# Selecting the first rows with a 0/1 matrix on TensorE instead of moving them by DMA, in the start of a convolution and feed-forward kernel

## The chip, the cores and the metric

The kernel runs on one core of one Trainium2 chip. The metric is the device time of one execution in microseconds (us). It was compared in rounds in which the kernel before and the kernel in question run in turn on the same chip. The profiled span is some 1.7 us shorter than the device time; spans are compared with spans only. "A draw" below is one profiled execution.

Engine names in the profile: PE is TensorE's matmuls, PEld its weight loads, DVE VectorE, ACT ScalarE, POOL GpSimd, SP SyncE; SPq and POOLq are where these two issue DMAs. "Block" is a piece of work of the main loop: block 0 and block 1 are one sub-block of 512 tokens each, later blocks are two.

## The reference, cut to what matters

```python
# attention-like part: a causal convolution whose 7 weights differ per token and head
w = softmax(weight_gen, axis=-1)               # (8, 4096, 8 heads, 7)
out[b, s, h*24 + g] = sum_k w[b, s, h, k] * x_pad[b, s + k, h*24 + g]   # D = 192
# feed-forward part on 32768 tokens
h = maximum(out @ w_in, 0.0)                   # w_in (192, 2048)
return (h * h) @ w_out                         # w_out (2048, 192)
```

## The kernel before: the parts that matter

The convolution is done as matmuls with banded matrices. For each sub-block there are five tiles of 128 rows of softmax weights (`wr`), laid one token to a partition. DVE multiplies them with a mask into bands (`bd`), and TensorE multiplies the bands with x. The softmax of the first 1024 tokens leaves its weights `v` with 8 tokens to a partition, so for block 0 small DMAs move the rows into tiles:

```python
def wr_load_sbuf(j, parts, order, engines):
    wr_t[j] = p_wr.tile([P, NT, HP, SL * 2], f16, name="wr")
    ...                                  # one DMA per tile, alternating over engines
        engines[n % len(engines)].dma_start(out=wr_t[j][..., i], in_=s.v[...])
```

A "unit" is 12 short matmuls (`h`, output 64x256) with 128 columns of w_in in blocks 0 and 1; ACT then applies ReLU (`t`), and DVE squares (`g`). A second copy of w_in with its halves of partitions exchanged (`w_i[:, q, 1]`) lets two row groups of the array work side by side. For the first half of the columns (q = 0) TensorE makes that copy with an exchange matrix; for the second half (q = 1) two DMAs, the "crossing", make it. Unit 4 is the first that needs the second half.

The start, in program order:

```python
spin(25)                                  # filler matmuls: they warm TensorE, no result
half_swap(); band_mask()
nc.gpsimd.memset(v_big, 0.0)
s0.load(nc.sync)                          # weight_gen of the first softmax
load_w_in(w_st[0], 0, nc.sync)            # first half of w_in, float32
x_load_f32(0)                             # x of block 0
load_w_in(w_st[1], 1, nc.sync)            # second half of w_in
... s0.exp / total / recip / scale        # v
nc.scalar.copy(out=w_i[:, 0, 0], in_=w_st[0])
wr_load_sbuf(0, [s0], (0, 2, 1, 4, 3), (nc.sync, nc.gpsimd))
wr_load_sbuf(1, [s0], range(NT), (nc.gpsimd,))
x_cast(0, nc.scalar.copy)
cross_w_in_by_pe(0)
spin(14)                                  # 14 more fillers
x_load_f32(1)
nc.scalar.copy(out=w_i[:, 1, 0], in_=w_st[1])
cross_w_in(1)                             # the crossing, by DMA
s1.load(nc.sync)
for i in (0, 2, 1, 3, 4):
    st_band(0, (i,))
st_conv(0)
nc.gpsimd.tensor_copy(out=gate, in_=x_st[1][:, 0:1])   # holds w_out back until x of block 1 is there
for q in range(4):
    load_w_out(q, 4)
```

The softmax here doesn't subtract the row's maximum and nothing guards it: scores larger than these inputs give would overflow.

## Time and profile before

| what | value |
|---|---|
| time, median of 3 runs | 736.59 us (735.5 to 736.84) |
| span in the profile, TensorE busy | 734.8 us, 725.9 us |
| first ReLU | 17.64 us |
| crossing issued / load of w_out issued | 14.01 / 15.37 us |
| unit 4 starts, its ReLU (the fifth) | 20.68 us, without a wait for data / 22.79 us |
| convolution of block 2 starts | 34.37 us |

The prediction below shows the page's totals, the waits and the timeline of the start. These are stretches of two microseconds of the kernel before; the columns are the stretch, its length, busy time and number of instructions of PE, PEld, DVE, ACT and POOL, the clock granted to TensorE (1.00 is full), the busy share of the 16 DMA engines and GB/s:

```profile
10.00:12.00 2.00, 2.00 (x10) 0.88 (x10) 0.00 (x0) 2.00 (x3) 2.00 (x5) 1.00 0.50 95
12.00:14.00 2.00, 1.97 (x21) 0.76 (x22) 1.23 (x3) 1.76 (x2) 0.22 (x1) 1.00 0.86 241
...
22.00:24.00 2.00, 1.62 (x26) 1.36 (x27) 1.93 (x6) 2.00 (x4) 0.00 (x0) 1.00 1.47 231
```

From 10 to 14 us TensorE is busy for all but 0.03 us, because of the 14 fillers and the matmuls of w_in's exchange, and the clock is full. From 22 us the DMA engines have more than they can do at once (a share over 1 means that packets overlap on an engine).

### The profile page before, as it was taken

How to read it: one execution, taken by the hardware profiler on the slowest of the kernel's cores; microseconds unless marked ns; L12 is line 12 of the kernel's file. 1: busy time of each engine (PE TensorE's matmuls, PEld its weight loads, DVE VectorE, ACT ScalarE, POOL GpSimd, SP SyncE). 2: the span in 40 equal slices, each digit the busy share in tenths (PEclk: the TensorE clock that was granted, in tenths of full speed). 3: DMA queues.
4: the chain of work that ended last, by engine and by line, in shares of the span. 5: the costliest groups of instructions: out<-in, count | busy, mean ns of one | idle time of the engine just before them, and what ended most of it. 6: DMA issues, size and time to landing. Idle time of an engine off the chain costs nothing.

```text
span 734.8 us, 31124 instructions
## 1 busy us (share of the span) xinstructions
PE 725.9 (99%) x14106; PEld 529.4 (72%) x14106; DVE 627.3 (85%) x856; ACT 613.5 (83%) x724; POOL 100.2 (14%) x148
## 2 busy tenths in 40 slices
PE   7999999999999999999999999999999999999998
PEld 3767777777767777777777777777777777777777
DVE  5999898998899988889888889888889888778853
ACT  4998888988888888888888888888888888888883
POOL 7322222320001100011000110010100110001000
PEclk9999999999999999999999999999999999999999
DMA  7846444794444533454433554334544315444012
GB/s 210 130 81 138 80 62 104 144 165 120 92 74 99 122 76 73 66 137 100 80 65 76 116 124 85 59 64 127 103 87 83 61 48 121 66 87 78 29 45 66
DMA packets 126544, 68.71 MB, mean 93 GB/s; under 512 B 85193, under 2 KB 122636, under 8 KB 125900
## 3 DMA queue, kind: packets, MB, share of 16 engines
q1 hardware_dynamic: 80908, 48.12, 22.9%
q0 software_dynamic: 45360, 18.50, 21.6%
q8 instruction: 110, 1.80, 1.0%
q14 instruction: 22, 0.18, 0.1%
q10 hardware_dynamic: 144, 0.10, 0.0%
HBM read 50.18 MB, written 28.70 MB: 107 GB/s over the span
## 4 chain that ended last, share of the span: by engine, by line
PE 70%; DVE 0%; ACT 0%; issue 0%
PE o L560 35%; PE h L518 32%; PE yp L450 3%; DVE g L536 0%; ACT o_sb L574 0%
## 5 line engine op out<-in xcount | busy, mean ns | idle before, releaser
L532 ACT ACTIVATE t<-h 128x1024 f16<-128x1024 f32 x512 | 496.4, 1026 | 60.1 <-PE h L518 59.7
L560 PEld LDWEIGHTS <-g 64*128 64x128 f16 (+1 forms) x8032 | 342.8, 94 | 56.9 <-issue 2.5
L560 PE MATMUL o<-w_o,g 64*128 64x192 f16 (+1 forms) x8032 | 379.7, 243 | 0.7 <-DVE g L536 0.6
L536 DVE TENSOR_TENSOR g<-t 128x2048 f16<-128x2048 f16 (+1 forms) x309 | 309.2, 1037 | 27.6 <-ACT t L532 27.3
L518 PE MATMUL h<-y,w_p 64*128 64x512 f16 x2400 | 291.7, 376 | 0.0
L518 PEld LDWEIGHTS <-w_p 64*128 64x128 f16 x2400 | 113.8, 94 | 94.8
L381 DVE TENSOR_TENSOR bd<-wr,mask 128x4160 f16<-128x4160 f16 (+3 forms) x89 | 149.4, 1703 | 4.7 <-DMA wr<-v_first 4.7
L576 DVE TENSOR_TENSOR o_sb<-o,o_sb 128x384 f32<-128x384 f32 x123 | 68.4, 556 | 62.1 <-ACT o_sb L574 61.3
L333 POOL DMA_DIRECT2D xt<-in_x_dram x62 | 52.1, 844 | 422.6 <-PE yp L450 363.7
L574 ACT COPY o_sb<-o 128x384 f32<-128x384 f32 x129 | 61.5, 477 | 48.0 <-PE o L560 47.5
L518 PE MATMUL h<-y,w_i 64*128 64x512 f16 (+1 forms) x768 | 82.3, 350 | 1.8 <-ACT t L532 0.8
L518 PEld LDWEIGHTS <-w_i 64*128 64x128 f16 x768 | 37.2, 94 | 27.7 <-issue 4.0
L450 PEld LDWEIGHTS <-xt 128*32 128x32 f16 x2000 | 24.4, 95 | 10.6 <-issue 10.6
L272 DVE TENSOR_TENSOR v_big<-ex,rcp 128x112 f16<-128x112 f32 (+5 forms) x180 | 29.9, 237 | 2.1 <-DMA vd<-v_big 1.1
L460 DVE CAST y<-yp 128x1024 f16<-128x1024 f32 x25 | 30.4, 1218 | 0.0
L450 PE MATMUL yp<-bd,xt 128*32 128x104 f16 (+1 forms) x2000 | 28.3, 209 | 0.0
L250 ACT ACTIVATE ex<-wg 128x560 f32<-128x560 f32 (+4 forms) x38 | 25.9, 682 | 1.7 <-DMA wg<-in_weight_gen_dram 1.7
L257 DVE TENSOR_REDUCE ssum<-ex 128x80 f32<-128x560 f32 (+4 forms) x38 | 25.3, 666 | 2.2 <-ACT ex L250 2.2
L460 ACT CAST y<-yp 128x1024 f16<-128x1024 f32 x25 | 25.2, 1007 | 0.0
L264 DVE RECIPROCAL rcp<-ssum 128x80 f32<-128x80 f32 (+4 forms) x38 | 22.8, 600 | 1.3
L323 POOL DMA_DIRECT2D xt<-in_x_dram x7 | 3.9, 555 | 124.7 <-PE yp L450 109.7
L363 POOL DMA_DIRECT2D wr<-v_first x31 | 16.9, 565 | 15.9 <-DVE v_first L272 15.7
(34 smaller groups left out, 95.8 us busy)
## 6 DMA issues: line engine op xcount, KB each, us to landing
out_dram<-o_sb SPq DMA_DIRECT2D x63, 384.0 KB
xt<-in_x_dram POOLq DMA_DIRECT2D x42, 240.0 KB, 5.1
wg<-in_weight_gen_dram SPq DMA_DIRECT2D x4, 1064.0 KB
xt<-in_x_dram POOLq DMA_DIRECT2D x20, 192.0 KB, 4.6
wr<-vd SPq DMA_DIRECT2D x38, 80.0 KB
vd<-v_big SPq DMA_DIRECT2D x5, 512.0 KB
y<-y SPq DMA_DIRECT2D x100, 24.0 KB
wg<-in_weight_gen_dram SPq DMA_DIRECT2D x5, 392.0 KB
```

The costliest lines, as they stand in the source:

```text
L250: nc.scalar.activation(out=self.ex[:, lo:hi].rearrange("p r g k e -> p (r g) k e"), in_=self.wg[:, lo:hi].rearrange("p r (g e) k -> p (r g ...
L272: eng.tensor_tensor(out=bass.AP(tensor=v.tensor, offset=v.offset + lo * H * SL + lo % SL * 2 + g * SL * 2, ap=[list(v.ap[0]), [H * SL + 2, ...
L333: eng.dma_start(out=dst[:, first:last], in_=ap)
L381: nc.vector.tensor_tensor(out=bd_t[j][:, H * lo : H * (lo + len(tiles) * n)].rearrange("p (g m c) -> p g m c", g=shape[1], c=2 * SL), in0= ...
L450: nc.tensor.matmul(out=yp[p0 : p0 + 32, k - k0, a:b], lhsT=x_t[s][:, i, c0 : c0 + 32], rhs=bd[:, head // 2, e, 0 : b - a], start=True, sto ...
L460: copy(out=y[:, k0 : k0 + 2], in_=yp)
L518: nc.tensor.matmul(out=h[:, half, jj * th : (jj + 1) * th], lhsT=w_in_chunk(w, u * per + jj, slot, half), rhs=y_t[j][r0 : r0 + RT, k, 0:th ...
L532: nc.scalar.activation(out=t1[:, e], in_=h, func=ActF.Relu)
L536: nc.vector.tensor_tensor(out=g[:, a : e + 1], in0=t1[:, a : e + 1], in1=t1[:, a : e + 1], op=AluOp.mult)
L560: nc.tensor.matmul(out=oo[:, cc * Dm : (cc + 1) * Dm], lhsT=g[r0 : r0 + n, cc * P : (cc + 1) * P], rhs=w_o[r0 : r0 + n, fc, :], start=(fc ...
L574: nc.scalar.copy(out=o_sb, in_=o[0][:, c])
L576: nc.vector.tensor_tensor(out=o_sb, in0=o[1][:, c], in1=o_sb, op=AluOp.add)
```

## The change

Intent: take the DMA between v and the bands away. A 0/1 matrix `sel` picks the rows: eight matmuls per tile, one for each of the eight tokens of a partition, add up in PSUM, and ACT copies the 128x64 result out. x is loaded ahead of w_in. DVE, which no longer waits for rows, casts the first half of w_in and copies all of y; the 14 fillers go; ACT's cast of the second half of w_in comes last. Cut to its core:

```diff
+    def row_select():
+        nc.gpsimd.affine_select(out=sel, in_=sel, pattern=[[-1, NSEL]], ..., fill=1.0,
+                                base=FIRST - 1, channel_multiplier=FIRST)
+    def select_rows(j, s, tiles):
+        ...
+        for i in tiles:
+            a = max(j % NBB * TB + tile_start(j, i), 0) - s.t0
+            for r in range(s.r):
+                c = a + FIRST - 1 - r
+                nc.tensor.matmul(out=pr_t[j][:, i], lhsT=sel[:, c : c + P],
+                                 rhs=s.v[:, HALO + r]..., start=(r == 0), stop=(r == s.r - 1), ...)
+            nc.scalar.copy(out=wr_t[j][:, i]..., in_=pr_t[j][:, i])
@@ st_conv
-                copies = ((0, 2, nc.scalar.copy), (2, NK, nc.vector.tensor_copy))
+                copies = ((0, NK, nc.vector.tensor_copy),)
@@ start
+        row_select(); band_mask()
         half_swap()
-        band_mask()
+        x_load_f32(0)
         load_w_in(w_st[0], 0, nc.sync)
-        x_load_f32(0)
         load_w_in(w_st[1], 1, nc.sync)
...
-        nc.scalar.copy(out=w_i[:, 0, 0], in_=w_st[0])
-        wr_load_sbuf(0, [s0], (0, 2, 1, 4, 3), (nc.sync, nc.gpsimd))
-        wr_load_sbuf(1, [s0], range(NT), (nc.gpsimd,))
         x_cast(0, nc.scalar.copy)
-        cross_w_in_by_pe(0)
-        spin(14)
         x_load_f32(1)
+        nc.vector.tensor_copy(out=w_i[:, 0, 0], in_=w_st[0])
+        wr_load_sbuf(1, [s0], range(NT), (nc.gpsimd, nc.sync))
+        s1.load(nc.sync)
+        select_rows(0, s0, (0, 2, 1))
+        cross_w_in_by_pe(0, 0, 2 * TB)
+        select_rows(0, s0, (3, 4))
+        cross_w_in_by_pe(0, 2 * TB, 3 * TB)
         nc.scalar.copy(out=w_i[:, 1, 0], in_=w_st[1])
         cross_w_in(1)
-        s1.load(nc.sync)
```

## The prediction

> **What bounds the kernel now.** I read the page's totals and the chain that ended last, then TensorE's waits before and after 26 us, then the timeline of the first 18 us.
>
> ```profile
> span 734.8 us, 31124 instructions
> PE 725.9 (99%) x14106; PEld 529.4 (72%) x14106; DVE 627.3 (85%) x856; ACT 613.5 (83%) x724; POOL 100.2 (14%) x148
> PE 70%; DVE 0%; ACT 0%; issue 0%
> ```
>
> TensorE works in 725.9 of 734.8 us and the chain that ended last lies on it. Only 8.9 us of the span are without a matmul. The waits of TensorE from 26 us to the end of the span:
>
> ```profile
> PE o L560 <- DVE g L536: 0.6, 2, 0.3
> ```
>
> and from 0 to 26 us (total us, times, longest):
>
> ```profile
> PE pt L149 <- ACT w_i L643: 1.3, 1, 1.3
> PE wp L624 <- DVE warm L616: 1.3, 1, 1.3
> PE h L518 <- ACT t L532: 0.8, 1, 0.8
> PE h L518 <- ACT y L503: 0.7, 1, 0.7
> PE yp L487 <- DVE bd L381: 0.3, 1, 0.3
> PE yp L487 <- DVE xt L347: 0.3, 1, 0.3
> ```
>
> After 26 us TensorE has 0.6 us of waits in 709 us, so what the start-up gains or loses is passed through to the end one for one, and nothing else in this change touches the steady part. The waits of the start look small because 39 filler matmuls (wp, 25 and then 14) hide them: they do no work for the result. The real question is when the first useful unit (h, L518) can run. The timeline of the start (start us, duration us, engine, line):
>
> ```profile
> 6.61 1.46 DVE L272 TENSOR_TENSOR v_first<-ex,rcp 128x112 f16<-128x112 f32 x8
> 8.38 1.47 ACT L643 CAST w_i<-w_st 128x1536 f16<-128x1536 f32 x1 [3.70 <-DMA w_st<-in_moe_w_in_dram]
> 9.90 0.99 ACT L347 CAST xt<-x_st 128x960 f16<-128x960 f32 x1
> 10.79 1.49 ACT L153 CAST w_i<-pt 128x1024 f16<-128x1024 f32 x2
> 12.51 1.47 ACT L650 CAST w_i<-w_st 128x1536 f16<-128x1536 f32 x1 [0.23 <-DMA w_st<-in_moe_w_in_dram]
> 12.77 2.60 DVE L381 TENSOR_TENSOR bd<-wr,mask 128x832 f16<-128x832 f16 x5 [4.71 <-DMA wr<-v_first]
> 14.93 0.94 PE L487 MATMUL yp<-bd,xt 128*32 128x104 f16 x46 [0.28 <-DVE bd L381]
> 15.90 0.59 ACT L503 CAST y<-yp 128x512 f16<-128x512 f32 x1 [1.91 <-PE yp L487]
> 16.52 0.42 DVE L503 CAST y<-yp 128x256 f16<-128x256 f32 x1 [1.14 <-ACT y L503]
> 16.54 3.04 PE L518 MATMUL h<-y,w_i 64*128 64x256 f16 x48 [0.68 <-ACT y L503]
> 17.64 2.85 ACT L532 ACTIVATE t<-h 128x1024 f16<-128x1024 f32 x3 [1.16 <-PE h L518]
> ```
>
> The softmax weights v are ready at 6.61 + 1.46 = 8.07. DVE then idles 4.71 us for the row-moving DMAs, builds five bands, TensorE convolves until 15.87, y is copied out, and the first ReLU starts at 17.64. That last moment is my yardstick. From v to the first ReLU it is 17.64 - 8.07 = 9.57 us, and 4.70 of it is the DMA. One of those issues, of 8 to 9 us (KB, us to landing):
>
> ```profile
> wr<-v_first POOLq DMA_DIRECT2D x1, 16.0 KB, 4.5
> ```
>
> **What the Trainium skill says.** (1) "DMA: Bandwidth & Descriptors", section "Anatomy of one DMA — SWDGE (gpsimd) path", puts a fixed cost of about 2.0 us on a DMA, mostly completion. The trace agrees in kind: 16 KB takes 4.5 us here behind other traffic, so size is not what costs. (2) "TensorE: Matmul & The Clock Gate", "Back-to-back issue gap", gives about 81 ns for a weight load and matmul pair at N=128. Here a 16-pair group with N=192 takes 1.49 us, 93 ns each; nothing as short as N=64 with 128 columns of weights is in this trace. (3) The same page, "What's actually happening", says the clock falls to half after an idle window of about 3.4 us. In the trace the first fillers are 0.43 us apart and from 4.7 us on 0.21, so warming is seen; falling back is not seen in this run. (4) "PSUM — Partial Sum Buffer", "PSUM bank collisions raise a hardware error", asks that a bank, not an address, be guarded between engines. The trace agrees that copies out of one PSUM tile are kept apart: DVE's part of y waited 1.14 us, until ACT's part was done, although the two read different columns.
>
> **The change part by part.**
> *Removed: five DMAs of rows of block 0, and 14 fillers.* That takes away DVE's 4.71 us wait. The fillers were only filling (3.18 us, none on the path).
>
> *Added: 40 selecting matmuls (8 per tile, N=64) and 5 ACT copies of 128x64 out of PSUM.* Matmuls: between 60 and 80 ns per pair by (2), I take 70: 8 x 0.07 = 0.55 us per tile. ACT copies from PSUM cost 589 ns for 512 columns and 1006 for 1024 in this trace, that is 0.17 us + 0.815 ns per column, so 0.22 us for 64. All five tiles lie in one PSUM bank (5 x 64 x 4 B = 1280 B), so by (4) the matmuls of the next tile wait for the copy of the last one. With 0.1 us per hand-over, a tile then costs 0.55 + 0.1 + 0.22 + 0.1 = 0.97 us, one after the other, not 0.55.
>
> *Order on the engines.* The 25 fillers end at 1.27 + 7.29 = 8.56, so tile 0 starts there. Tile 1, the third, has its matmuls done at 8.56 + 2 x 0.97 + 0.55 = 11.05. Then two crossing matmuls (N=512, 0.22 each): 11.5. ACT copies their 1024 columns: 11.6 + 1.0 = 12.6; only then, in order, tile 3: 12.8. Tile 4: 12.9 + 0.55 + 0.1 + 0.22 = 13.8. Its band on DVE (0.59 mean of L381): 14.5. The convolution ended 0.49 after the last band (15.87 against 15.37): 15.0.
>
> *y by DVE alone.* DVE takes 424 ns for 256 columns from PSUM and 1218 for 1024, so 1.03 ns per column and 0.95 us for 768: 15.95. Before, the two copies in turn ended at 16.94, which is 1.07 after the convolution: about equal. From there the first ReLU came 17.64 - 16.94 = 0.70 later, so now at 16.65. Gain 17.64 - 16.65 = 1.0 us.
>
> *x ahead of w_in; casts moved.* x is 491 KB, each half of w_in 786 KB, weight_gen 401 KB. Over 2 to 10 us the queues moved about 290 GB/s. w_in's first half landed at 8.38; x put ahead delays it by at most 491/290 = 1.7 us, to 9.3 (they overlapped before) or 10.1. DVE's cast of 1536 columns is 653 ns x 1536/960 = 1.05 us, so done by 10.4 to 11.2. The crossing matmuls ask for it at 11.05, so this is nearly hidden. DVE's bands 0, 2, 1 stand behind this cast, but they have until 12.8. The ACT cast of x (0.99 us) goes to about 6 us, where ACT idles: hidden. What it saves is the 1.47 + 0.99 us that ACT spent ahead of the crossing copies, without which the copies of tiles could not be this early.
>
> *Second half of w_in.* ACT's cast moves behind tile 4's copy and the last crossing copy (0.59): 13.8 + 0.6 + 1.47 = 15.9 instead of 13.98. Its two DMAs are issued 1.9 us later.
>
> Sum: 4.7 us of DMA wait go, about 3.7 us come back as the select-copy chain with a crossing copy in its middle (v to last band, 8.07 to 14.5, instead of 8.07 to 15.37, with 0.49 of it spent on fillers). Net about -1.0 us, passed on: 736.6 - 1.0 = 735.6; I say 735.5.
>
> **Rivals.**
> A. *The tiles are not held apart by the bank.* Then tiles cost 0.55 each, tile 1's matmuls end at 10.2 and all is 0.9 us or more earlier: about 734.3. Against it: the wait of DVE's y for ACT's.
> B. *The clock falls back.* Between 8.56 and 16 us the full 512-column fillers are gone and TensorE has short matmuls with gaps of under 1 us. For: less work per us than before. Against: no gap near 3.4 us, and a 1.35 us gap at 8.56 did no harm before. If it fell, the first units (0.76 us each) would take 1.5, against 1.0 us of ReLU per unit: 1 to 1.5 us lost, about 736.8.
> C. *The second half of w_in comes late.* Unit 4 ran at 20.68 and is now wanted at 19.7; its DMAs, issued 15.9 to 17.1, may land at 19.5 to 20.5. But ACT only took that unit at 22.79, 1.3 us after it ended, so the wait is mostly absorbed: 0 to 0.5 us.
> D. *w_in's first half is later than 10.1.* DVE stands at its cast with the bands behind it, so each us beyond 10.1 costs nearly one us. With 3 us late the gain is gone. Against: the queue moves 1.68 MB (weight_gen, x, first half) by 8 us at the rates seen.
> E. *Rows of block 1 late.* POOL now has the larger selecting mask to make before its memset, so its DMAs start perhaps 1 to 2 us later and land at 14.5 to 15.5; they are wanted at 15.95. Within the slack.
>
> **Range and chances.** My sum gives -1.0 with about 0.5 either way from the pair time (60 or 80 ns: 24 to 32 pairs on the path, 0.3 us each way) and the hand-overs; A is worth up to -2.3, B to D up to +0.8. The three runs of before spread over 1.3 us themselves. So 735.5, with 734.0 to 737.0 for 8 in 10. 2% is 14.7 us, more than the whole start-up from v to the first ReLU (9.57 us), so neither side of it is in reach without a fault: 0.01 each.
>
> **What would show it.** The wait of 4.71 us on wr gone from DVE. Five groups of 8 selecting matmuls about 1 us apart (A: 0.55). An ACT copy of 0.22 us after each, the fourth standing behind a 1.0 us crossing copy. DVE's last band at 14 to 15 us, and the first ReLU at 16.65. The granted clock at 1.00 throughout, matmuls of L518 of 256 columns at about 269 ns as now (B: longer). After 26 us no new wait of TensorE. I am wrong if the first ReLU is not earlier, or is earlier by over 2 us, or if the steady part changes its length.

## The result, and the profile after

| | before | after |
|---|---|---|
| median of 6 runs each, same rounds | 736.25 us (735.49 to 738.67) | 738.39 us (737.74 to 739.45) |
| mean granted clock | 1.000 in the profiled run; 0.998 to 1.000 in the later rounds | 0.995 to 0.997 in the six runs |
| span in the profile | 734.8 us | 736.8 us |

The ratio is 1.0027, with a 95% interval of 1.001 to 1.0044. Ratios here are the mean time of one kernel's fast runs over that of the other's of the same rounds, so they are not quite the ratio of the medians. Within 2% it is the same time, as predicted, but the sign is wrong: the kernel is slower by about 2 us, and 738.39 lies above the predicted range.

The waits of TensorE in the kernel after, from 0 to 26 us (total, times, longest):

```profile
PE h L542 <- DMA w_i<-w_i: 2.2, 1, 2.2
PE pr L388 <- ACT wr L393: 1.6, 3, 1.0
...
PE h L542 <- DVE y L527: 1.0, 1, 1.0
PE pt L157 <- DVE w_i L671: 1.0, 1, 1.0
```

The first line was not there before: a unit waits 2.2 us for the crossing. The second is the hand-over between selecting matmuls and ACT's copies, as predicted. The last is TensorE waiting for DVE's cast of w_in. The timeline of the kernel after:

```profile
8.42 0.40 PE L388 MATMUL pr<-v_first,sel 128*128 128x64 f16 x8
...
9.11 0.39 PE L388 MATMUL pr<-v_first,sel 128*128 128x64 f16 x8 [0.30 <-ACT wr L393]
...
10.14 0.98 DVE L671 CAST w_i<-w_st 128x1536 f16<-128x1536 f32 x1 [2.00 <-DMA w_st<-in_moe_w_in_dram]
...
11.80 1.01 ACT L161 CAST w_i<-pt 128x1024 f16<-128x1024 f32 x1 [1.35 <-PE pt L157]
...
14.67 3.05 POOL L202 DMA_DIRECT2D w_o<-in_moe_w_out_dram  x4
...
15.61 1.21 SPq L150 DMA_DIRECT2D w_i<-w_i  x2
...
16.65 2.85 ACT L556 ACTIVATE t<-h 128x1024 f16<-128x1024 f32 x3 [1.07 <-PE h L542]
...
19.66 0.51 PE L542 MATMUL h<-y,w_i 64*128 64x256 f16 x3
...
22.36 1.89 PE L542 MATMUL h<-y,w_i 64*128 64x256 f16 x16 [2.19 <-DMA w_i<-w_i]
...
23.64 1.02 ACT L556 ACTIVATE t<-h 128x1024 f16<-128x1024 f32 x1 [1.71 <-PE h L542]
```

A tile of selection takes 0.39 us of matmuls and 0.30 us of waiting. The first ReLU starts at 16.65 us, exactly the number predicted, 0.99 us earlier than before. Then unit 4 begins at 19.66, 1.02 us earlier than before, runs three matmuls and stands until 22.36. The fifth ReLU starts at 23.64 where it was 22.79. So between the first and the fifth ReLU 1.84 us were lost, and the gain of 0.99 became a loss of 0.85. Note the two DMA issues: the load of w_out (14.67) now leaves ahead of the crossing (15.61); before, the crossing was 1.36 us ahead.

The clock in the same draw (columns as above):

```profile
10.00:12.00 2.00, 1.03 (x17) 0.60 (x14) 1.86 (x3) 0.41 (x2) 0.33 (x1) 1.00 1.06 236
...
20.00:22.00 2.00, 0.17 (x1) 0.00 (x0) 1.97 (x3) 1.93 (x3) 0.00 (x0) 0.97 1.44 214
22.00:24.00 2.00, 1.64 (x16) 1.17 (x18) 1.97 (x10) 0.36 (x1) 0.00 (x0) 0.50 1.32 302
```

TensorE now works only 1.03 of 2.00 us between 10 and 12. After the standstill at 20 to 22 us the clock is at half, and the units right after it take twice as long. That adds another 0.36 us: the convolution of block 2 starts at 35.58 instead of 34.37, 1.21 later. The other 0.7 us to the end of the span are a stall in block 7 (block 8 is 1.63 late; a matmul wait of 0.23 us put down to "issue" is seen in it) and 0.30 us more between the issue of the last output and the end of the span (2.74 us and 2.44; second draws 2.75 and 2.45). What causes that last part stays open.

Who had the DMA engines? Of the kernel before, the queues (packets, MB, share of 16 engines) from 15 to 17 us, while its crossing was on the way:

```profile
q1 hardware_dynamic: 171, 0.43, 94.3%
```

and of the kernel after, from 17 to 18 us, with its crossing issued 1.4 us before:

```profile
q0 software_dynamic: 480, 0.18, 151.6%
```

Queue q1 carries what SyncE issues, the crossing among it; q0 what GpSimd issues, w_out among it. Before, q1 had the engines alone. After, 480 packets of q0, all under 512 bytes and nearly all of them w_out's, fill them and no packet of q1 moves in that microsecond. The crossing landed 6.75 us after its issue. Its 128 packets can be told by their size (3072 bytes; the two kernels below that do without this DMA have none): before, they moved from 15.19 to 17.02 us, and the first packet of w_out only at 17.83; after, w_out's began at 16.19 and the crossing's moved from 18.13 to 21.75, between them.

### The profile page after: what moved, and what is told of

Same layout as the page of the kernel before. It is cut to its first block, busy times and chain, and to the rows that moved or that the text cites. A ratio compares the mean times of both kernels' runs of the same rounds, so it can differ in the third digit from the quotient of the medians.

```text
span 736.8 us, 31175 instructions
## 1 busy us (share of the span) xinstructions
PE 725.0 (98%) x14132; PEld 530.6 (72%) x14132; DVE 630.0 (86%) x858; ACT 613.0 (83%) x727; POOL 98.3 (13%) x145
## 4 chain that ended last, share of the span: by engine, by line
PE 70%; DVE 0%; ACT 0%; issue 0%
PE o L584 34%; PE h L542 32%; PE yp L474 3%; DVE g L560 0%; ACT o_sb L598 0%
## 5 line engine op out<-in xcount | busy, mean ns | idle before, releaser
L371 POOL DMA_DIRECT2D wr<-v_first x27 | 14.8, 567 | 14.8 <-DVE v_first L280 11.5
```

## The experiments

First suspicions: (1) the crossing stands behind w_out; (2) the missing fillers cost clock; (3) w_in's first half comes late because x is ahead of it; (4) the selection itself. Each kernel is told by its edit against the kernel after, if not said otherwise. Runs told together shared a chip and the runs of the kernel before.

### First four: the order of w_out and the crossing, and the rows by DMA again

Hold the load of w_out until the crossing has landed, by letting GpSimd read one element of its result:

```diff
         nc.gpsimd.tensor_copy(out=gate, in_=x_st[1][:, 0:1])
+        nc.gpsimd.tensor_copy(out=gate, in_=w_i[:, 1, 1, 0:1])
```

> The changed kernel, but GpSimd starts loading w_out only when the second half of w_in has been crossed (landed). Theory (the crossing DMA shares the DMA engines with the w_out load, whose small packets are ahead of it, and so takes 6.75 us from issue to unit 4): the crossing lands by about 18 to 18.5 us, TensorE no longer waits 2.2 us for it at unit 4, the granted clock stays 1.00 from 20 to 26 us, unit 4 runs at about 19.7, and the first product with w_out comes at 25.5 us unless w_out itself is now late (issue at 18.5 plus 6 to 7 us: 25). Total near 735.5 us, 2.5 to 3 us under the changed kernel. Rival (the crossing is late only because ACT's cast is 1.6 us later, and a DMA takes its 6 to 7 us whatever else runs): unit 4 still starts at 22.4, total as the changed kernel or later.

The same, but only until ACT has cast the second half of w_in, so that w_out is issued just behind the crossing:

```diff
+        nc.gpsimd.tensor_copy(out=gate, in_=w_i[:, 1, 0, 0:1])
```

> The changed kernel, but the w_out load is held until ACT's cast of the second half of w_in is done (15.6 us), so that it is issued about together with the crossing DMA, not 0.9 us ahead of it. Theory of shared DMA engines: the crossing gets part of its 0.39 MB through before the w_out packets come, lands at about 19 to 20.5 us, TensorE's wait for it shrinks from 2.2 us to under 1, the clock stays at 1.00; total about 736. Rival (only the late cast counts): no change, about 738.4.

Fillers in the place where TensorE waited for the crossing:

```diff
                     st_conv(j + 1)
                     if j == 0:
+                        spin(11)
```

> The changed kernel with 11 filler matmuls of 512 columns (0.216 us each, 2.4 us) between the convolution of block 1 and unit 4, where TensorE otherwise waits for the crossing. Theory (the loss at the start has two parts: the wait itself, and a clock at half from 22 to about 25 us that the idle time brings on): the crossing still lands at about 22.4, but the granted clock stays 1.00, units 4 to 7 run at 0.83 us each; total 0.5 to 1.2 us under the changed kernel, that is about 737.5. Rival (the low clock comes from the thin work between 8.6 and 16 us, not from this wait; or it is free because ACT's ReLUs bound these units): same total as the changed kernel within 0.3 us, with or without a low clock.

And the rows of block 0 by DMA again, with the rest of the change kept:

```diff
+        wr_load_sbuf(0, [s0], (0, 2, 1, 4, 3), (nc.sync, nc.gpsimd))
-        select_rows(0, s0, (0, 2, 1))
         cross_w_in_by_pe(0, 0, 2 * TB)
-        select_rows(0, s0, (3, 4))
```

> The changed kernel with the selection by TensorE undone: the rows of block 0 come by five DMAs again; x stays ahead of w_in, the casts stay moved. Theory (the selection saves the DMA wait, 1 us of it net): DVE waits for rows until about 12.8 us, bands end at about 15.4, the first ReLU starts at about 17.7 (changed kernel 16.65), the crossing of the second half is issued about 0.7 us earlier than 15.6. Rival (the move of x and of the casts, not the selection, brought the first ReLU forward): first ReLU at 16.7 to 17. With TensorE nearly idle from 8.6 to 11 us the clock may fall before the first units: then below 1.00 somewhere in 11 to 18 us.

Measured, against 736.06 us of the kernel before on this chip:

| kernel | median us | ratio (95%) | clock of its runs |
|---|---|---|---|
| w_out after the crossing landed | 741.05 | 1.0067 (1.0055 to 1.008) | 0.993 to 0.995 |
| w_out after the cast | 739.03 | 1.0042 (1.0029 to 1.0054) | 0.993 to 0.995 |
| fillers in the wait | 741.14 | 1.0065 (1.0052 to 1.0079) | 0.992 to 0.995 |
| rows by DMA | 744.97 | 1.0114 (1.01 to 1.0128) | 0.990 to 0.993 |

The crossing did become quick. From the timeline of the first of these, the crossing's issue and the gate that waits for its landing:

```profile
16.95 1.15 SPq L150 DMA_DIRECT2D w_i<-w_i  x2
...
20.56 0.27 POOL L685 CAST gate<-w_i 128x1 f32<-128x1 f16 x1 [5.14 <-DMA w_i<-w_i]
```

It took 3.6 us instead of 6.75, and in both kernels that hold w_out unit 4 no longer waits for it. So suspicion (1) is shown as far as the wait goes. But the time did not fall, for two reasons that these draws show. w_in's first half came later than in the first draw: DVE's cast began at 10.68, 11.40 and 11.62 us in the first three, against 10.14. And the clock fell early: in the first of them it was 0.50 in all stretches from 12 to 20 us, in the second from 13.5 to 20.3, in the third from 12.2 to 22.4, before the place in which its fillers were put. That kernel therefore tested nothing about the wait; its fillers were a miss. Two causes were now mixed into every run, and the fillers had to be put back first.

### Next four: the fillers

The kernel before without its 14 second fillers, and nothing else (against the kernel before):

```diff
         cross_w_in_by_pe(0)
-        spin(14)
```

> The kernel before with nothing changed but its 14 filler matmuls taken out. Theory C (the clock: the fillers kept TensorE dense enough between 8.6 and 13.7 us; without them the granted clock falls to half for several us while the first units run): granted clock of the span 0.993 to 0.997 where it was 1.000, half clock beginning between 11 and 17 us, the first four units at over 0.9 us each in place of 0.76, total 2 to 4 us over before. Theory D (what the prediction said: the fillers only filled, none on the path; the loss of the changed kernel is the crossing DMA behind the w_out load): same total as before within 0.3 us, clock 1.000.

The kernel after with 13 fillers in the gaps of its start:

```diff
         select_rows(0, s0, (0, 2, 1))
+        spin(5)
         cross_w_in_by_pe(0, 0, 2 * TB)
-        select_rows(0, s0, (3, 4))
+        select_rows(0, s0, (3,))
+        spin(4)
+        select_rows(0, s0, (4,))
...
         st_conv(0)
+        spin(4)
```

> The changed kernel with 13 fillers put back in the three places where TensorE waits anyway: 5 after the first three selections, 4 between the fourth and the fifth, 4 between the convolution and the first unit (0.216 us each). Theory C: the clock does not fall before 20 us in any run; where the crossing is still late TensorE waits about 2 us at unit 4 and the clock may fall there, as in the changed kernel's profile. Total about 736.5 to 737.5, clock 0.997 to 1.000. Theory D: no change, 738.4, since the wait for the crossing is left.

That, and w_out held until the cast of the second half (the gate as above):

> Both cures: the 13 fillers of the run before and the w_out load held until ACT's cast of the second half of w_in is done. If C and the shared DMA engines each cost their part: clock 1.000, no wait of TensorE at unit 4 over 0.5 us, first ReLU at 16.6 to 17.2, total about 1 us under before, near 735.2. If only C: as the run before. If only D: as the changed kernel with the hold alone, 739.

And the rows by DMA as above, with 26 fillers (8, 14 and 4):

> The changed kernel without the selection (rows by DMA) but with 26 fillers (8 ahead of the crossing matmuls, 14 after, 4 ahead of the first unit). Theory C: of the 8.9 us that rows by DMA without fillers lost against before (745.0), most was the clock; with fillers the clock is 1.000 and the total is within 1.5 us of before, 736 to 737.5. Compared with the run that has selection and fillers it gives what the selection alone is worth: about 1 us. If it stays over 740, the cost is elsewhere (rows that land later behind the x and w_in loads).

Measured, against 736.3 us of the kernel before:

| kernel | median us | ratio (95%) | clock of its runs |
|---|---|---|---|
| before without 14 fillers | 737.67 | 1.0024 (1.001 to 1.0037) | 0.995, once 0.992 |
| after + 13 fillers | 737.37 | 1.0021 (1.0009 to 1.0034) | 0.998 to 1.000 |
| that + w_out held | 738.13 | 1.0029 (1.0017 to 1.0042) | 0.999 to 1.000 |
| rows by DMA + 26 fillers | 743.02 | 1.0094 (1.008 to 1.0108) | 0.996 to 1.000 |

The kernel before without its fillers, in stretches of 2 us:

```profile
12.00:14.00 2.00, 1.36 (x62) 1.03 (x62) 1.81 (x4) 0.68 (x1) 0.54 (x2) 0.80 0.94 271
14.00:16.00 2.00, 1.33 (x34) 0.97 (x25) 0.80 (x2) 0.59 (x1) 1.36 (x3) 0.50 0.99 230
```

and its first units, from its timeline:

```profile
15.22 5.13 PE L518 MATMUL h<-y,w_i 64*128 64x256 f16 x48 [0.67 <-ACT y L503]
```

The same 48 matmuls take 5.13 us instead of 3.04, at the same line. Nothing else was touched: the "fillers" kept the clock, and removing them alone costs 0.24%, where the whole change costs 0.27% and, measured again below, 0.39%. Suspicion (2) is shown for the clock and for the units under it. How much of the 0.24% it is, is less clear. In that draw the rows happened to land early: the first ReLU came at 16.75, 0.89 us ahead of before, and the convolution of block 2 was only 0.15 ahead, so the half clock cost about 0.7. Another 0.8 us was lost in blocks 3 and 6, at full clock, in stalls that are told of at the end of the experiments.

With fillers the kernel after keeps its clock, and is still slower than before. In that draw w_in's cast began at 11.61 and the first ReLU at 18.11, later than before's 17.64. In the one with w_out held the cast began at 11.00, the first ReLU at 17.50. With the first draw (10.14 and 16.65) that makes the first ReLU follow the cast by 6.5 us in the three draws with x first and selection in which the clock is full. So (3) is on the path, one for one. Holding w_out cured unit 4's wait again, and the convolution of block 2 started 0.15 earlier than before; but then the rows of block 2, now behind w_out, made TensorE wait 0.5 us, and block 3 was 0.87 late. The wait had moved.

The selection is not the culprit: with the same load order and with fillers in both, it takes 737.37 us (13 fillers) where rows by DMA take 743.02 (26). By DMA the rows landed at 15.46 us, behind the loads that now come first. So (4) falls: in this load order the selection is worth 5.6 us.

### Next four: two repeats, and w_in first again

The two kernels again, unchanged, to see what differs between draws:

> The kernel before once more, unchanged, for a second profile on the chip of the runs that follow. If its start is as steady as its times: w_in's first half cast from about 8.4 us, rows waited for until 11 to 13 us, first ReLU at 17.6 within 0.3 us (the 14 fillers end at 13.7 and hold the convolution back to that moment even where the rows come early), clock 1.000, ratio 1.000.

> The changed kernel once more, unchanged. Theory D (x ahead of w_in makes w_in's first half land at 10 to 12 us, from draw to draw, and everything behind its cast on DVE moves with it): cast on DVE begins at 10 to 12 us and the first ReLU 6.5 us after that at full clock, more at half clock. Theory C (clock): 0.995 to 0.997 again, half clock beginning at 11 to 13 us where the cast is later than 10.5. Rival (the first profile is the typical one): cast at 10.1, first ReLU at 16.65, clock falling only at 21 us.

The kernel after with w_in's first half ahead of x again, x cast by DVE, and 10 fillers spread thinly:

```diff
-        x_load_f32(0)
         load_w_in(w_st[0], 0, nc.sync)
+        x_load_f32(0)
...
-        x_cast(0, nc.scalar.copy)
-        x_load_f32(1)
         nc.vector.tensor_copy(out=w_i[:, 0, 0], in_=w_st[0])
+        x_cast(0, nc.vector.tensor_copy)
+        x_load_f32(1)
...      # and spin(1) after tiles 0 and 2, spin(4) after tile 3, spin(4) behind st_conv(0)
```

> The changed kernel with w_in's first half loaded ahead of x again, as in before, x cast by DVE behind w_in's cast, and 7 fillers in gaps. Theory D: the cast of w_in begins at 7 to 8.6 us, as in before, the crossing matmuls no longer wait for it, last band at about 13.3, first ReLU at 15.4 to 16, 1.5 to 2 us earlier than before; clock 0.999 to 1.000. Total: unit 4 is then wanted at about 18.5 and the crossing (issued at about 15) may be late by 1 to 2 us, so 735.0 to 736.5. Rival (the order of the loads does not matter, w_in lands when the queue is empty): cast again at 10 to 12 us, total as the run with fillers alone, 737.4.

In that load order, all five selections ahead of the exchange matmuls, so that no copy of a tile stands behind an exchange copy on ACT (10 fillers again):

```diff
-        select_rows(0, s0, (0, 2, 1))
+        ...                                # tiles 0, 2, 1, 3, 4 with spin(1) between them
         cross_w_in_by_pe(0, 0, 2 * TB)
-        select_rows(0, s0, (3, 4))
         cross_w_in_by_pe(0, 2 * TB, 3 * TB)
+        spin(2)
...      # and spin(4) behind st_conv(0)
```

> As the run before, but all five selections ahead of the crossing of w_in's first half, with a filler after each of the first four and two after the crossing. A selected tile takes 0.70 us in the profile, so five end at 8.5 + 3.5 = 12.0; last band at 12.6, convolution done at 13.1, y at 14.1, first ReLU at 14.7 to 15.2. If the 1 us crossing copy between tile 3 and tile 4 was on the path, this is 0.6 to 0.8 us better than the run before; if not, equal. The total can show it only if unit 4 does not wait longer in turn: 734.3 to 736.

Measured, against 736.62 us:

| kernel | median us | ratio (95%) | clock of its runs |
|---|---|---|---|
| before again | 736.03 | 0.9996 (0.9983 to 1.0009) | 1.000, once 0.998 |
| after again | 739.72 | 1.0039 (1.0027 to 1.0051) | 0.993 to 0.995 |
| w_in first | 737.4 | 1.0018 (1.0 to 1.0036) | 0.998 to 1.000 |
| w_in first, selection first | 737.55 | 1.0014 (1.0002 to 1.0026) | 1.000, twice 0.997 |

The second draw of the kernel after is a different story from its first: here the clock falls early.

```profile
12.00:14.00 2.00, 1.02 (x14) 0.52 (x10) 1.37 (x4) 1.28 (x3) 0.00 (x0) 0.75 1.16 265
14.00:16.00 2.00, 1.53 (x73) 1.42 (x73) 0.99 (x2) 1.84 (x2) 1.30 (x3) 0.50 0.42 124
16.00:18.00 2.00, 1.41 (x14) 1.18 (x15) 2.00 (x2) 0.12 (x1) 2.00 (x4) 0.50 0.88 92
```

The 48 matmuls of the first units take 4.35 us instead of 2.80, the first ReLU comes at 18.09, and the crossing's wait is only 0.2 us, because the units reach it late. The fifth ReLU: 23.66 here, 23.64 in the first draw. Two different causes end at the same place.

Why did one kernel lose its clock at 13.0 us in one draw and at 21.9 in the other? The clock records of the traces show a grid: in all 20 draws every change up to 40 us lies a whole number of 3.41 us after the moment when the clock first became full (4.83 us in the first draw, 6.16 in the second). Here are two stretches of that grid from the first draw, and one from the second:

```profile
8.24:11.65 3.41, 1.84 (x30) 1.20 (x29) 1.51 (x3) 0.64 (x3) 2.09 (x4) 1.00 1.04 253
18.48:21.89 3.41, 1.46 (x77) 0.99 (x75) 3.38 (x6) 3.41 (x5) 0.68 (x1) 1.00 1.38 215
...
9.57:12.99 3.42, 1.61 (x26) 1.09 (x26) 2.47 (x4) 1.63 (x5) 0.80 (x2) 1.00 1.08 253
```

The clock fell at the end of the last two, not of the first. Over all draws it fell nine times, each time after a stretch in which TensorE was busy for 0.93 to 1.61 us. It held after all others (1.84 us and more) but one of 1.54 us (in "all together" below), so busy time is not the whole measure. Where the grid lies differs from draw to draw, and so the same gaps can cost the clock or not.

(The expectation of "w_in first" says 7 fillers; 10 were built. One of its six runs took 741.06 us.) With w_in first, DVE's cast began at 8.16 and 8.22 us without a wait, and the first ReLU came at 15.79 and, with the selections first, at 15.47: 1.9 and 2.2 us earlier than before. And yet unit 4 waited for the crossing until 21.13 and 21.19, and the fifth ReLU came at 21.88 and 21.95. Two us of lead at the first ReLU had shrunk to 0.9 at the fifth. The first ReLU was the wrong yardstick.

### Next three: what takes the crossing's place

w_in first and nothing else, so without fillers (the diff of "w_in first" above, less its `spin` lines):

> The changed kernel with only the order of the loads undone (w_in's first half ahead of x; x cast by DVE behind it), without fillers. Theory: w_in's cast starts at 8.2, TensorE does not wait for it, first ReLU at 15.8 to 16.5 if the clock holds that long. Without fillers the clock falls again in most runs (0.995 to 0.998), at half from 12 to 16 us on. Total 737 to 738.5: better than the changed kernel on the same chip by 1 to 2 us, worse than the same with fillers (737.4, spread 736.0 to 741) by 0 to 1. Rival (w_in's landing is not what hurts): total as the changed kernel, 739.

The exchanged copy of the second half loaded from HBM by four casting DMAs of GpSimd, in the load order of the kernel after:

```diff
+    def cross_w_from_hbm(q):
+        c = q * NQ
+        for p0, r0 in ((0, RT), (RT, 0)):
+            nc.gpsimd.dma_start(out=w_i[p0 : p0 + RT, q, 1, 0:NQ], in_=moe_w_in[r0 : r0 + RT, c : c + NQ])
+        for p0, c0 in ((0, c + NQ // 2), (RT, c)):
+            nc.gpsimd.dma_start(out=w_i[p0 : p0 + RT, q, 1, NQ:], in_=moe_w_in[P:D, c0 : c0 + NQ // 2])
...
+        cross_w_from_hbm(1)            # behind the loads of the rows of block 1
-        cross_w_in(1)
```

> The changed kernel with only the crossing of w_in's second half replaced: its crossed copy is loaded straight from HBM by four casting DMAs of GpSimd at about 10.3 to 12.5 us, so it depends on no cast and meets no w_out load. Theory (the crossing behind the w_out load is one part of the loss): no wait of TensorE at unit 4; total 0.5 to 1.2 us under the changed kernel (739.7 on the last chip, 738.4 on the first), less where the half clock has already made the first units late so that the wait was small (0.2 us in the second profile). Rival: the extra 0.39 MB delays the rows and x of block 1 by as much, no gain.

And that together with w_in first, the selections first and the fillers:

> All three cures: loads in the old order, fillers, selections first, and the second half crossed straight from HBM. If the three causes are all there is: first ReLU at 15.5, no wait at unit 4, clock 1.000, convolution of block 2 at 32.3 to 32.9 (before 34.0 to 34.4), total 734.8 to 735.5, 1 to 1.5 us under before. If the time is given back in the later blocks as in the last two runs (0.4 to 0.8 us between 75 and 160 us), 735.5 to 736.5.

Measured, against 736.01 us:

| kernel | median us | ratio (95%) | clock of its runs |
|---|---|---|---|
| w_in first only | 738.0 | 1.0024 (1.0006 to 1.0041) | 0.997 to 1.000 |
| crossing from HBM | 739.36 | 1.0047 (1.0035 to 1.0059) | 0.993 to 0.995 |
| all together | 737.92 | 1.0025 (1.0013 to 1.0037) | 1.000, once 0.998 |

With w_in first only, the first ReLU is at 15.56, unit 4 waits 2.3 us, and after this wait the clock falls as in the first draw of the kernel after (0.50 in 22 to 24 us). One of its six runs kept the full clock; it took 735.39 us, the other five 737.59 to 739.18. From HBM the crossing is never waited for, but in the load order of the kernel after the clock falls as before (half from 11.4 to 21.7 us). In all together the clock is full, the crossing is in time, the first ReLU is at 16.38 — and now the rows of block 1 are late: DVE waits for them until 18.10, its cast of x of block 1 stands behind, and the convolution of block 1 waits 2.8 us, until 21.09. The lead went into a different DMA. The busy share of the DMA engines between 12 and 24 us, in stretches of two, was 1.00 to 1.54 in this kernel: there is no free stretch into which one more early load would fit.

### Last three: the best version, and a delay on purpose

w_in first, the selections first, fillers, and the second half of w_in cast by DVE behind the bands instead of by ACT, so that the crossing is issued sooner:

```diff
-        nc.scalar.copy(out=w_i[:, 1, 0], in_=w_st[1])
-        cross_w_in(1)
...      # behind the five st_band(0, (i,)), ahead of st_conv(0) and spin(4)
+        nc.vector.tensor_copy(out=w_i[:, 1, 0], in_=w_st[1])
+        cross_w_in(1)
```

> The run with old load order, fillers and all selections first, with one more change: w_in's second half is cast by DVE in its 1.08 us of idle time ahead of y (at about 12.5 us), not by ACT at 13.4 to 14.9, so the crossing is issued at about 13.6 in place of 14.9, ahead of the w_out load (14.0). Theory (unit 4 is the second deadline of the start: whatever the first ReLU gains is lost unless the crossing, which lands when the DMA engines have let it through, comes earlier too): crossing lands by 19 to 20, fifth ReLU at 20.5 to 21.5 where it was 21.95 (22.4 in before), convolution of block 2 about 0.5 to 1 us earlier than 33.5; total 735.0 to 736.5. Rival (the start is bound by all the DMA traffic together, not by the order of the crossing and the w_out load): fifth ReLU again at about 21.9, or x and rows of block 1 late instead; total 737 to 738 as the three runs before.

That with w_out held until y of block 0 is copied:

```diff
+        nc.gpsimd.tensor_copy(out=gate, in_=y_t[0][:, 0, 0:1])
```

> The run before with the w_out load held until y of block 0 is there (about 14.5 us), so that it follows the crossing's issue by about 1.1 us as in before (1.36 us). Theory: crossing lands by 18 to 19, no wait at unit 4, fifth ReLU at 20 to 20.8; but rows for blocks 2 and 3 come later behind w_out, as in the run with fillers and hold, which lost 1 us between 34 and 55 us. Total 735 to 737. Rival as above: no gain.

And the kernel before with 14 fillers on the path, between the convolution of block 0 and the first unit, to see whether a delay in the start is passed on (against the kernel before):

```diff
         st_conv(0)
+        spin(14)
```

> The kernel before with 14 more fillers (3.0 us) between the convolution of block 0 and the first unit, of which about 0.7 us lie in TensorE's own wait: the first unit starts about 2.3 us later and nothing else is changed. It tests the step of the prediction that the steady part passes the start on one for one. If so: convolutions of block 2 and block 8 both 2.3 us later, total +2.3 us, 738.4. If the stretch from 40 to 160 us takes up differences (another deadline that does not move with the start, as four kernels suggest that came to block 3 0.3 to 1.3 us early and to block 8 within 0.13 us of before): the delay at block 8 is clearly smaller than at block 2, total +1 to +1.5 us. If earliness is lost to stalls that lateness meets as well: the delay at block 8 is 2.3 us or more.

Measured, against 736.05 us (the first two) and 736.42 us:

| kernel | median us | ratio (95%) | clock of its runs |
|---|---|---|---|
| w_in first, DVE casts | 736.61 | 1.0002 (0.9989 to 1.0015) | 0.999 to 1.000 |
| that + w_out held | 736.93 | 1.0011 (0.9999 to 1.0024) | 0.999 to 1.000 |
| before + 14 on the path | 738.26 | 1.0026 (1.0012 to 1.0039) | 0.999 to 1.000 |

With DVE's cast the crossing was issued at 14.30 and nothing waited for it; the fifth ReLU came at 21.56 and the convolution of block 2 at 33.15, 1.22 us ahead of before. With w_out held it came at 32.20, 2.17 ahead. But the time is that of the kernel before. Where did this lead go? The start of each block's convolution, as its difference from the kernel before (us):

| kernel | block 2 | block 3 | block 4 | block 5 | block 7 | block 8 |
|---|---|---|---|---|---|---|
| before again | -0.39 | -0.38 | -0.39 | -0.39 | -0.45 | -0.46 |
| w_in first, DVE casts | -1.22 | -1.21 | -1.21 | -0.55 | -0.29 | -0.07 |
| that + w_out held | -2.17 | -1.25 | -1.26 | -0.41 | -0.03 | +0.05 |
| before + 14 on the path | +0.97 | +0.97 | +0.97 | +0.97 | +1.73 | +1.72 |
| after | +1.21 | +1.21 | +1.20 | +1.18 | +1.15 | +1.63 |

(With 14 fillers on the path the first ReLU was 0.98 late, not 2.3 as expected: in that draw the first convolution had begun 0.68 us earlier than before's.) A delay is passed on in full, and some more is added in blocks 6 or 7. A lead of 1.2 us is lost between blocks 4 and 8 (with w_out held, 0.9 of the 2.17 already in block 2, half of it in a wait for x). Part of the loss is seen as a stall, here in the first of these kernels:

```profile
79.16 0.50 PE L584 MATMUL o<-w_o,g 64*128 64x192 f16 x7 [0.40 <-issue]
```

"Issue" says that the engine waited for nothing that the profile shows. It is not a fixed deadline: before's second draw keeps its lead of 0.4 us and starts block 8 at 158.48, and no other kernel of the table reached that.

The kept traces say more about these stalls. The page of each kernel has a queue for instructions:

```profile
q8 instruction: 110, 1.80, 1.0%
```

That is 110 packets of 16 KB, and TensorE has 14,106 matmuls and as many weight loads in the kernel before: one packet for each 256 of them. Counted along these two, the "issue" waits of all eight kernels that have one after 38 us (0.2 to 0.6 us, at 79 to 85 us and 125 to 149 us) stand at number 2752, 4544 or 5568, which lie 7 and 4 times 256 apart, and TensorE goes on 1.25 to 1.45 us after a packet of q8 has ended. In all 20 draws no block of 256, counted like this, began sooner than 1.2 us after its packet. So TensorE most likely waits there for its own instructions. At 134 to 138 us there is another kind, in five kernels: TensorE waits for DVE, here in the kernel before with 14 on the path:

```profile
136.06 1.48 PE L560 MATMUL o<-w_o,g 64*128 64x192 f16 x31 [0.54 <-DVE o_sb L576]
```

The kernel after, which is late, loses 0.4 us where such a block of instructions begins, too, and "before without 14 fillers" 0.8 at two of them. So it is not only a lead that is taken up: these kernels meet stalls that before does not. The change and each filler more or less shift the matmul at which a block begins; whether that or the DMA traffic of the moment makes a block late, no run separates.

## Why the prediction was right or wrong

**Right.** The 4.71 us wait for rows went. The hand-over of one PSUM bank is there (three waits, 1.6 us), so rival A fell; rival E did not come (DVE began the bands of block 1 at 15.66 us without a wait); the copies of ACT took 0.21 us (0.22 predicted), DVE's copy of y 0.96 us (0.95). In the first profile the first ReLU came at 16.65 us, as predicted. Class "same" was right as well.

**Mis-sized: "a tile then costs ... 0.97 us".** It took 0.70: eight pairs 0.39 us instead of the 0.55 estimated from the page's figure, and 0.30 us from matmul to matmul through ACT. That the first ReLU still came out at 16.65 is luck, because another term was too small by about as much: the crossing matmuls began at 11.17 after a wait of 0.97 us for DVE's cast, where the prediction had them start after tile 1 at 11.05.

**Failed: "x put ahead delays it by at most 491/290 = 1.7 us" (rival D).** With x first the cast of w_in began at 10.11 to 11.62 us in all ten draws of this load order. With w_in first it began at 7.22 to 8.38 us in the draws of the kernels that kept before's start. The prediction had it landing at 9.3 to 10.1. The delay is thus between 1.7 us (10.11 - 8.38) and 4.4 us (11.62 - 7.22), not at most 1.7. That each microsecond beyond 10.1 "costs nearly one us" was right (first ReLU = cast + 6.5 us); the mean rate of 290 GB/s said nothing about the order in which the bytes of three loads on one queue arrive.

**Failed: "The fillers were only filling (3.18 us, none on the path)".** Taken out alone they cost the kernel before a ratio of 1.0024 at a clock of 0.995 (part of it, as said, in later stalls at full clock). A mean clock of 0.995 is about 0.005 x 736 x 2 = 7 us at half speed, which is what the windows show. The kernel after ran at 0.993 to 0.997 in all timed runs. I had rival B on the list and argued it away with "no gap near 3.4 us": in the second draw of the kernel after the clock fell at 13.0 us, and no gap of TensorE between 8 us and that moment was over 1.0 us. The same page that I quoted, "TensorE: Matmul & The Clock Gate" of the Trainium skill, says so in another section, "A second HAM failure mode: psum-queue depth-cycling": TensorE that idles briefly but often between groups of matmuls swings between half and full clock. That section describes this start, tiles handed over through PSUM, better than the one I used; the trace agrees that short idle times are enough (busy 1.61 of 3.42 us, no gap over 1.0, clock 0.50 from 13.0), but shows one fall and one rise, not repeated swings. What the fillers did is raise that busy time: in the start of the kernel before no stretch of the grid had less than 2.07 us.

**Failed: "the wait is mostly absorbed: 0 to 0.5 us" (rival C).** In the first profile it was 2.2 us, with slower units behind it. Issue at 15.9 to 17.1 and landing at 19.5 to 20.5 allowed the crossing some 3.5 us. That is what it takes when w_out is held back (3.6), and the issue came even sooner, at 15.61. But the order of two issues had flipped: w_out was 1.36 us behind the crossing and is now 0.94 us ahead, and beside it the crossing took 6.75 us. (Nothing waited for before's, but its last packet ended 3.0 us after the issue; with w_out held it was 2.9, in the kernel after 6.1.) The mechanism of the rival was right, the flight time was the term that was mis-sized.

**Failed: "so what the start-up gains or loses is passed through to the end one for one".** Losses are, with more added (14 fillers on the path: +0.97 at block 2, +1.72 at block 8). Gains were lost in two parts. In the start, the first ReLU reached 15.47 us, 2.2 earlier than before (w_in first, selections first), and 0.9 of it was left at block 2, because the next things needed are DMAs too: the crossing for unit 4, then rows and x of block 1, then rows and x of block 2. Later, what was left at block 2 (1.22 us with DVE's cast) held to block 4 and then went in three stalls: about 0.6 us at 79 us and 0.2 at 147, both where a block of instructions began, and 0.3 at 134, where TensorE waits for DVE. "Nothing else in this change touches the steady part" fell with it: the kernel after, late from the start, lost 0.4 us there as well. Before's lack of waits after 26 us showed that TensorE was bound in that kernel; it did not show that the changed one would have no waits, or the data a microsecond earlier.

So the slower 1.9 us of the first profile are: a gain of 0.99 at the first ReLU; 1.84 lost between the first and the fifth ReLU, by the wait for the crossing (in the second draw late w_in and half clock end at the same place); another 0.36 by the clock after the wait; 0.41 from block 2 to the last output, nearly all in block 7; 0.30 behind the last output: -0.99 + 1.84 + 0.36 + 0.41 + 0.30 = 1.92, which is 736.75 - 734.84. The first three terms are explained by the runs. The fourth falls where a block of instructions begins, as read from the traces and not tested by a run; the last stays open. No version here beats the kernel before; the best (w_in first, selections first, fillers, DVE's cast) equals it at 1.0002, and its interval lies below that of the kernel after's second measurement.

## What to carry to other kernels

Before matmuls that compute nothing are removed, take them out alone and look at the granted clock: fillers are part of the clock's upkeep, and short matmuls with waits between them do not replace them. When a load is moved ahead in a start where the DMA engines are full, list who is now behind it and when each is needed, and check whether the order of two issues on different queues flips. After a gain at one point, the yardstick is the next consumer that is fed by a DMA, not the point itself. A path without waits in one kernel does not show that the changed kernel has none: compare the starts of later blocks in both.

## What the Trainium skill lacked or had wrong

- "TensorE: Matmul & The Clock Gate", "What's actually happening" and "A second HAM failure mode: psum-queue depth-cycling": neither says how busy TensorE must be to keep its clock. The first says that it falls after an idle window of about 3.4 us. Here the stretches of 3.41 us after which it fell were not idle: TensorE was busy 0.93 to 1.61 us of them, with matmuls in every one and in the second draw no gap over 1.0 us. With 1.84 us and more the clock held (and once with 1.54). It came back after stretches with 2.62 us and more, and stayed at half after those with 2.56 and less.
- Same page, "Back-to-back issue gap": its spacing of weight load and matmul pairs starts at N=128 (its row for 1 to 64 columns is for single matmuls). Eight pairs at N=64 with 128 columns of weights took 0.39 to 0.40 us here, 49 ns a pair.
- "DMA: Bandwidth & Descriptors", "Anatomy of one DMA — SWDGE (gpsimd) path": a fixed cost near 2.0 us plus the bytes does not size a DMA where queues compete. A DMA of 16 KB by GpSimd took 4.5 us in the kernel before. No page gives a time for one like the crossing (SyncE issues it, 2 x 192 KB within SBUF): it took 6.75 us beside the load of w_out, and 3.6 us with it held back.
- Same page, "Queues, rings and completion order": it says that an engine takes turns between its queues, a packet from each. In the kernel after, queue q0 moved 480 packets from 17 to 18 us and q1 none, with a DMA of q1 issued at 15.61. Its first packet moved at 18.13, 2.5 us after the issue, where it was 1.2 us in the kernel before. Whether q1 had nothing ready yet or did not get its turn, the runs do not tell.
- "Runtime: NRT & Kernel Launch", "Instruction fetch mechanics": it has no time for what TensorE loses when a block of its instructions comes late. The waits put down to "issue" here, 0.2 to 0.6 us in eight of the kernels, all stand where such a block begins, 1.25 to 1.45 us after its packet ended.
